# One-core linear attention, mixture of experts and MLP: another opening order, routing sums and one-hots on GpSimd, earlier second gather

## The chip, the cores and the metric

One Trainium2 chip, of which the kernel uses one core. The metric is the device time of one execution in microseconds (us). TensorE (PE) multiplies, VectorE (DVE) and ScalarE (ACT) work on elements and can read the matmul results in PSUM, GpSimd (POOL) works on elements in SBUF and issues the indirect DMAs, SyncE (SP) issues nearly all other DMAs. Each engine takes its instructions in the order in which the program lists them, and a waiting instruction holds back all behind it on that engine or queue.

## The reference

```
proj = x @ w_phi                            # x is q or k; 4 batches, 8 heads, 576 rows, 64 wide
phi(x) = [exp(proj - max|proj|), exp(-(proj - max|proj|))]       # 128 + 128 features
kv = sum_s phi(k)[s] v[s]^T ;  z = sum_s phi(k)[s]
x  = phi(q) @ kv / (phi(q) @ z + 1e-6)      # regrouped to 2304 tokens x 512
noisy  = x @ w_gate + log1p(exp(x @ w_noise)) * noise            # 8 experts
top2   = the two largest of noisy ; weights = softmax over the two
out    = sum over the two experts e of weight * (relu(x @ w1[e]) @ w2[e])   # 512 -> 1024 -> 512
result = max(0.01 h, h) @ w_out,  h = out @ w_in                 # 512 -> 2048 -> 512
```

## The kernel before

**Attention.** It goes by 16 pairs i (a batch b and two of its heads; four pairs are a batch), each over 576 rows as nine tiles in three chunks c. One turn of the main loop (i = 0 to 16) does, in PE's order: `proj` of q (chunk by chunk) and of k for the next pair, as fp16 high and low products into one of three shared PSUM banks (L309, L310, tile `pj`); `kv`, nine tiles per head (L348); transposes of the subtracted q (L334, `tq`); two `fold` products; and the numerators of the pair before (L200, tiles nA, nb). Between them DVE takes the row maximum (L312) and the difference (`shk`, `shq`, L315), ACT the two exponentials `ke` of a k chunk (L327), the copy `kvs` of the finished kv of one head (L356) and the copies `qT`, and DVE divides and forms the gate sums at the pair's end (L410 to L424). The copy `kvs` of head 0 comes once per pair and serves below as the clock of the attention.

**Raw inputs.** q, k and v come as "doubles" of two pairs on SP's queue (`load_double`); the first pair of all comes by itself. Raw q or k of a pair is split into an fp16 high part (`splk`, `splq`: ACT L281, or L294 by thirds) and a low part (POOL L282, or the engine handed in, L295), and then transposed: for most pairs by one DMA on SP's queue (`split_one`, L284, tiles `stkk`, `stkq`), for the first tiles by PE and three ACT copies (`split_pe`, L299, L301).

**Routing.** Per batch a generator `Route` produces the routing in small steps. `tick()` takes the next step of the generator at the head of a list (`flow`); a `yield n` asks for n more ticks before the next step, `PE_NEXT` waits for a place where the routing's own matmuls may stand. The steps are: gate logits and noise scale; the noisy logits `nl` and the top two (`oh`, `ky`, `a`); the ranks of the tokens within their experts (matmuls `pr`, then `re`, `hi`, `lo`); the totals (`pc`, `a_sum`, `bump`, `ebase`); and two tables by one-hot products: for each (tile, choice) pair two one-hots, 128x128 from `lo` (L627) and 128x144 from `hi` (L632), five buffers, then matmuls `pt` (or `o`, L641) that add up which token stands in which slot. Batches 0, 1, 2 are put on the list after turns 4, 8, 12; the last batch is routed during the first steps of the experts. `index_columns` turns table columns into row indices `t_idx`.

**Experts and MLP.** The work is a list of steps s: `mm1` (L963) and `mm2` (L1009), in triples of fp32r high and low products. The first two blocks take the tokens of experts 0 and 1 that are known early. `fetch` gathers 128 rows of x by an indirect DMA on POOL's queue into one of three buffers `xg` (L759); `prep` transposes them (L795) and splits them. The buffers `xg` also hold the hidden values hh and hl of step 0. Weights are split into w0h, w1h (ACT L734) and w0l, w1l (L737: DVE, but the `w1l` of early steps POOL). The order between engines is written out by hand; nothing is scheduled for the author.

Of the kernel before, what the change touches and what calls it, by code (L numbers as in the profile page):

```python
# [26 lines left out]
def attention_moe_mlp_kernel(  # L27
# [259 lines left out]
    def split_pe(nm, i, eng):  # L287
# [14 lines left out]
        stk[nm, i] = x  # L302
# [20 lines left out]
    def k_exp(i, c):  # L323
# [4 lines left out]
        ke[i, c] = e  # L328

# [124 lines left out]
    class Route:  # L454


        def __init__(self, b):
            self.b, self.sb = b, rt_p
            g, odd = divmod(b, 2)
# [56 lines left out]
        def top2(self):  # L516
# [13 lines left out]
            for c in range(2):  # L530
# [5 lines left out]
                nc.vector.tensor_tensor(out=ky, in0=ky,  # L536
# [13 lines left out]
            nc.vector.tensor_tensor(out=a, in0=oh[:, 0], in1=oh[:, 1], op=ALU.add)  # L550
# [3 lines left out]
        def ranks(self):  # L554
# [16 lines left out]
            nc.vector.tensor_tensor(out=oh, in0=oh,  # L571
# [19 lines left out]
        def totals(self):  # L591
# [57 lines left out]
        def weights(self):  # L649
            J, t0 = self.J, self.t0  # L650
            dm = self.small([J], "dm")
            nc.vector.tensor_tensor(out=dm, in0=self.mx[:, 1], in1=self.mx[:, 0],
# [5 lines left out]
            nc.vector.tensor_scalar(out=dm, in0=ex, scalar1=1.0, scalar2=1e-9, op0=ALU.add,  # L658
# [633 lines left out]
```

## Time and profile before

| | us |
|---|---|
| median of 3 runs | 1134.14 (1133.57 to 1135.4) |
| profiled execution | 1134.5 |
| its span in the trace | 1132.7 |
| PE busy in it | 1085.3 (96%) |
| DVE, ACT, POOL busy | 732.6, 542.0, 218.8 |
| mean granted TensorE clock | 0.987 |

The attention ends at about 231 us, the experts and the MLP fill the rest. Times below are microseconds from the start of the span; an instruction's row gives its start and its length, and in brackets how long its engine was idle before it and which instruction ended that.

### The profile page before, as it was taken

Reading aid. Unit: us, or ns where it says so; the run is one execution under the profiler, and the core shown is the slowest. Engines: PE = TensorE matmul, PEld = TensorE weight load, DVE = VectorE, ACT = ScalarE, POOL = GpSimd, SP = SyncE. Lnnn points to the kernel's source line nnn. Section 1 sums busy time; section 2 is a strip of 40 time slices with the busy share of each in tenths; the row PEclk is TensorE's granted clock in tenths of the full one; section 3 lists DMA queues with packets and bytes.
Section 4 is the critical chain, followed back from the end, with each engine's and each line's share of the span. In section 5 each row is a group of like instructions: output and inputs, shape, how many; then the busy total and the mean of one; then the engine's idle time right before and its main releaser. Section 6 shows DMA issues by size and latency. Waiting matters only on the chain. (4 is left out here: it accounts for less than half of the span.)

```text
span 1132.7 us, 18128 instructions
## 1 busy us (share of the span) xinstructions
PE 1085.3 (96%) x6767; PEld 954.9 (84%) x6767; DVE 732.6 (65%) x1558; ACT 542.0 (48%) x1084; POOL 218.8 (19%) x248
## 2 busy tenths in 40 slices
PE   6899899989999999999999999889999999999998
PEld 5899899988888988888888888778888888888886
DVE  4568777779487767676667665576545645645443
ACT  6466455534456444444444454555444444444443
POOL 4121111105434315141413230330000000000000
PEclk9999899989999999999999999899999999999999
DMA  5856462535568636464545462202003003001001
GB/s 136 187 122 152 104 149 43 183 99 176 185 203 253 216 117 206 143 208 147 184 125 200 121 209 76 100 1 94 1 1 112 1 1 110 3 1 32 7 1 37
DMA packets 117001, 125.86 MB, mean 111 GB/s; under 512 B 61040, under 2 KB 87696, under 8 KB 116912
## 3 DMA queue, kind: packets, MB, share of 16 engines
q1 hardware_dynamic: 110320, 104.13, 32.4%
q0 software_dynamic: 6272, 20.03, 5.1%
q8 instruction: 54, 0.88, 0.3%
q10 hardware_dynamic: 320, 0.52, 0.1%
q14 instruction: 35, 0.29, 0.1%
HBM read 96.71 MB, written 19.40 MB: 103 GB/s over the span
## 5 line engine op out<-in xcount | busy, mean ns | idle before, releaser
L963 PE MATMUL m<-xth,w0l 128*128 128x304 f32 (+5 forms) x800 | 268.9, 336 | 3.3 <-issue 3.3
L963 PE MATMUL m<-xth,w0h 128*128 128x304 f32 (+5 forms) x800 | 265.4, 332 | 0.0
L963 PE MATMUL m<-xtl,w0h 128*128 128x304 f32 (+5 forms) x800 | 264.5, 331 | 0.0
L1009 PE MATMUL o<-w1l,hh 128*128 128x512 f32 (+1 forms) x608 | 241.0, 396 | 0.0
L1009 PE MATMUL o<-w1h,hh 128*128 128x512 f32 (+1 forms) x608 | 240.6, 396 | 0.0
L1009 PE MATMUL o<-w1h,hl 128*128 128x512 f32 (+1 forms) x608 | 239.8, 394 | 0.0
L963 PEld LDWEIGHTS m<-xth,w0l 128*128 128x128 f32 x800 | 151.3, 189 | 16.9 <-issue 3.7
L963 PEld LDWEIGHTS m<-xtl,w0h 128*128 128x128 f32 x800 | 151.3, 189 | 13.8
L963 PEld LDWEIGHTS m<-xth,w0h 128*128 128x128 f32 x800 | 151.3, 189 | 10.4
L1009 PEld LDWEIGHTS o<-w1h,hh 128*128 128x128 f32 (+1 forms) x608 | 113.1, 186 | 28.6
L1009 PEld LDWEIGHTS o<-w1h,hl 128*128 128x128 f32 (+1 forms) x608 | 113.1, 186 | 24.3 <-DVE hl L976 0.2
L1009 PEld LDWEIGHTS o<-w1l,hh 128*128 128x128 f32 (+1 forms) x608 | 113.4, 186 | 21.5
L973 DVE SCALAR_TENSOR_TENSOR g<-g 128x512 f32<-128x512 f32 (+1 forms) x80 | 53.4, 668 | 111.7 <-ACT g L972 111.6
L348 PE MATMUL kv<-ke,vs 128*65 128x128 f32 x640 | 121.5, 282 | 0.0
L972 ACT ACTIVATE g<-m 128x512 f32<-128x512 f32 (+1 forms) x80 | 44.4, 555 | 133.1 <-PE m L963 132.8
L734 ACT ACTIVATE w1h<-w2r 128x512 fp32r<-128x512 f32 x88 | 55.4, 630 | 84.0 <-PE o L1009 46.8
L967 DVE SCALAR_TENSOR_TENSOR hl<-m,hh 128x304 fp32r<-128x304 f32 (+4 forms) x128 | 57.9, 471 | 54.4 <-ACT hh L966 53.8
L312 DVE TENSOR_REDUCE m<-pj 128x3 f32<-128x384 f32 x96 | 52.9, 551 | 58.1 <-PE pj L310 57.8
L737 DVE TENSOR_TENSOR w1l<-w2r,w1h 128x512 fp32r<-128x512 f32 x72 | 49.7, 690 | 59.1 <-ACT w1h L734 55.0
L966 ACT ACTIVATE hh<-m 128x304 fp32r<-128x304 f32 (+4 forms) x128 | 50.5, 417 | 72.1 <-PE m L963 70.8
L976 DVE TENSOR_TENSOR hl<-g,hh 128x512 fp32r<-128x512 f32 (+1 forms) x80 | 51.1, 639 | 52.4 <-ACT hh L975 49.8
L975 ACT ACTIVATE hh<-g 128x512 fp32r<-128x512 f32 (+1 forms) x80 | 47.1, 589 | 68.3 <-DVE g L973 68.3
(187 smaller groups left out, 1762.5 us busy)
## 6 DMA issues: line engine op xcount, KB each, us to landing
w1r<-in_moe_w_dram SPq DMA_DIRECT2D x44, 512.0 KB, 4.8
w2r<-in_moe_w_dram SPq DMA_DIRECT2D x44, 512.0 KB, 3.8
y<-y_dram SPq DMA_DIRECT2D x18, 512.0 KB, 6.5
raw<-in_moe_w_in_dram SPq DMA_DIRECT2D x16, 512.0 KB, 4.0
raw<-in_moe_w_out_dram SPq DMA_DIRECT2D x16, 512.0 KB, 4.5
rawk<-in_k_dram SPq DMA_DIRECT2D x16, 256.0 KB, 4.6
vs<-in_v_dram SPq DMA_DIRECT2D x32, 128.0 KB, 3.2
x_dram<-xb SPq DMA_DIRECT2D x4, 1024.0 KB
```

The source lines that it names most:

```text
L312: nc.vector.tensor_reduce(out=m, in_=p, axis=AX, op=ALU.max, apply_absolute_value=True)
L348: nc.tensor.matmul(kvb[:, sg, h], vs[i // 2 % NV][:, i % 2, 5 * h + n], ke[i, t // 3][:, t % 3, sg], start=(n == 0), stop=(n == 4))
L734: nc.scalar.activation(hi, src, ACTF.Copy)
L737: (nc.gpsimd if pool else nc.vector).tensor_tensor(out=lo, in0=src, in1=hi.bitcast(F32), op=ALU.subtract)
L963: nc.tensor.matmul(p, w[:, kk], x[:, kk, c0:c1], start=(kk == 0 and m == 0), stop=(kk == KD - 1 and m == 2))
L966: nc.scalar.activation(hh[:, c0:c1], p, ACTF.Relu)
L967: nc.vector.scalar_tensor_tensor(out=hl[:, c0:c1], in0=p, scalar=0.0, in1=hh[:, c0:c1].bitcast(F32), op0=ALU.max, op1=ALU.subtract)
L972: nc.scalar.activation(g, p, ACTF.Copy)
L973: nc.vector.scalar_tensor_tensor(out=g, in0=g, scalar=0.01, in1=g, op0=ALU.mult, op1=ALU.max)
L975: nc.scalar.activation(hh[:, c0:c1], g, ACTF.Copy)
L976: nc.vector.tensor_tensor(out=hl[:, c0:c1], in0=g, in1=hh[:, c0:c1].bitcast(F32), op=ALU.subtract)
L1009: nc.tensor.matmul(acc[n][0:rows], a[:, c], w, start=(f == 0 and m == 0), stop=(f == nf - 1 and m == 2))
```

## The change

Four things move; the line numbers after the change are a few higher than before.

The opening: `split_pe` becomes a generator that is taken in pieces by `take`. The low part of q of pair 0 goes in front of the first exponentials, the exponentials of the third k chunk of pair 0 go behind the first `kvs` and `qT`, and the low parts of k of pair 1 are POOL's instead of DVE's. The loads of k of pair 1 stay early; the rest of double 1 (raw q, the rest of k, v) now stands in SP's queue behind the DMA transposes of q(1) and k(2). Doubles are loaded one turn-pair later, k is split two pairs ahead instead of three, the noise is loaded in turn 1 instead of 0, and some POOL memsets move into the middle of turn 0.

Routing: two more places that tick (`k_exp`, `kv_evac`) make 23 ticks per turn of 18. For the batches 0 to 2 GpSimd does both one-hots of a pair in one step, and the small sums and products listed in the diff.

Early gathers: the indices of expert 1's early tiles are made after batch 2's routing, and the gather of block 1 reads only the rows of x that batches 0 to 2 write.

```diff
@@ split_pe
+        stk[nm, i] = x
         for w in parts:
             nc.scalar.activation(s[:, w, 0], r[:, w], ACTF.Copy)
             eng.tensor_tensor(out=s[:, w, 1], in0=r[:, w], in1=s[:, w, 0], op=ALU.subtract)
+            yield
         for w in parts:
...
             nc.scalar.activation(x[:, w], p, ACTF.Copy)
-        stk[nm, i] = x
+            yield
@@ k_exp, kv_evac
+        tick()
@@ Route
+            self.eng = nc.gpsimd if b < B - 1 else nc.vector
...
-            nc.vector.tensor_tensor(out=nl, in0=sc, in1=nz[:, t0:t0 + J], op=ALU.mult)
+            self.eng.tensor_tensor(out=nl, in0=sc, in1=nz[:, t0:t0 + J], op=ALU.mult)
             # likewise nl + logits, ky * erev, a, oh * re, hi (two), a_sum +=,
             # max of bump, ebase +=, dm (two), wgt
...
-                nc.vector.tensor_scalar(out=ol, in0=iota[:, 0:128],
+                self.eng.tensor_scalar(out=ol, in0=iota[:, 0:128],
                                         scalar1=self.lo[:, c, j:j + 1], scalar2=None,
                                         op0=ALU.is_equal)
-                yield 0
                 t = self.t0 + j
-                nc.vector.tensor_scalar(out=oi, in0=iota, scalar1=self.hi[:, c, j:j + 1],
+                self.eng.tensor_scalar(out=oi, in0=iota, scalar1=self.hi[:, c, j:j + 1],
                                         scalar2=tokval[:, t, c:c + 1], op0=ALU.is_equal,
                                         op1=ALU.mult)
@@ fetch
-    N_EARLY = tile_of(2, 0)[0] * 128
+    def n_rows(bi):
+        if bi < len(EARLY_TILES):
+            t, p0, n = tile_of(1 + bi, 4)
+            return t * 128 + p0 + n if p0 == 0 else tile_of(2 + bi, 0)[0] * 128
+        return NT
...
-                out=x[0:m], out_offset=None, in_=x_dram[0:N_EARLY] if bi == 0 else x_dram,
+                out=x[0:m], out_offset=None, in_=x_dram[0:n_rows(bi)],
@@ opening
+    load_k(1, 0)
+    load_k(1, 2)
...
-    split_pe("k", 0, nc.vector)
+    k0 = split_pe("k", 0, nc.vector)
+    take(k0, 6)
+    q0 = split_pe("q", 0, nc.gpsimd)
+    take(q0, 3)
     for c in range(2):
         proj("k", 0, c)
-        k_exp(0, c)
-    split_pe("q", 0, nc.gpsimd)
+    k_exp(0, 0)
+    take(q0, 1)
+    k_exp(0, 1)
+    take(q0, 2)
     proj("k", 0, 2)
-    k_exp(0, 2)
     load_gates()
@@ route
-        if b == 1:
-            flow.append([0, index_columns((0, EARLY_TILES[0]))])
+        if b > 0:
+            c = (b - 1) * TPE
+            flow.append([0, index_columns((c, c + EARLY_TILES[b - 1]))])
@@ main loop
             if i == 0:
-                split_pe("k", 1, nc.vector)
-                load_double(1)
+                k_exp(0, 2)
+                k1 = split_pe("k", 1, nc.gpsimd)
+                take(k1, 3)
+                split_one("q", 1)
+                take(k1, 3)
+                load_q(1)
+                split_one("k", 2)
+                load_k(1, 1)
+                for part in range(3):
+                    load_v(1, part)
...
-            split_one("q", 1)
-            split_one("k", 2)
-            load_double(2)
-            load_noise()
-        if i + 3 < NPAIR:
-            split_one("k", i + 3)
+            for n in range(1, NV):
+                make_ones(n, nc.gpsimd)
+            make_pads()
+        if 0 < i < NPAIR - 2:
+            split_one("k", i + 2)
...
-        if i % 2 and (i + 5) // 2 < NPAIR // 2:
-            load_double((i + 5) // 2)
+        if i % 2 and (i + 3) // 2 < NPAIR // 2:
+            load_double((i + 3) // 2)
@@ after the attention
-    flow.append([0, index_columns((TPE, TPE + EARLY_TILES[1]))])
     flow.append([0, iter_fetch(1)])
```

ACT in the opening, before: raw q split (`splq`, three thirds) stands behind four exponentials, all six exponentials of pair 0's k before the first `kvs`, and the splits of q(1), k(2), k(3), q(2) before the second.

```order
L327 ACTIVATE ke<-shk 128x3x128 x4
L294 ACTIVATE splq<-rawq 128x3x64 x3
L301 ACTIVATE stkq<-tr 128x384 x3
L327 ACTIVATE ke<-shk 128x3x128 x2
L356 ACTIVATE kvs<-kv 65x256
L338 ACTIVATE qT_128<-tq 128x3x2x64 x2
L294 ACTIVATE splk<-rawk 128x3x64 x3
L301 ACTIVATE stkk<-tr 128x384 x3
L327 ACTIVATE ke<-shk 128x3x128 x2
L281 ACTIVATE splq<-rawq 128x9x64
L281 ACTIVATE splk<-rawk 128x9x64 x2
L281 ACTIVATE splq<-rawq 128x9x64
```

ACT in the opening, after, from the same place:

```order
L295 ACTIVATE splq<-rawq 128x3x64 x3
L329 ACTIVATE ke<-shk 128x3x128 x2
L303 ACTIVATE stkq<-tr 128x384
L329 ACTIVATE ke<-shk 128x3x128 x2
L303 ACTIVATE stkq<-tr 128x384 x2
L359 ACTIVATE kvs<-kv 65x256
L341 ACTIVATE qT_128<-tq 128x3x2x64 x2
L329 ACTIVATE ke<-shk 128x3x128 x2
L295 ACTIVATE splk<-rawk 128x3x64 x3
L281 ACTIVATE splq<-rawq 128x9x64
L303 ACTIVATE stkk<-tr 128x384 x3
L281 ACTIVATE splk<-rawk 128x9x64
```

The split of q moved ahead of all exponentials, two exponentials moved behind `kvs` and `qT`, and one whole split (q(1)) now stands between the thirds of k(1) and their copies. Behind these rows stand two `ke`, the split of q(2) and the second `kvs`, in both.

SP's queue in the opening, before: all of double 1, the two transposes of q(1) and k(2), then double 2.

```order
L225 DMA rawq<-in_q_dram 128x2x576
L238 DMA rawk<-in_k_dram 128x2x256
L254 DMA vs_123<-in_v_dram 128x4x64 x4
L259 DMA vs_123<-in_v_dram 64x2x64 x2
L284 DMA_TRANSPOSE stkq<-splq 128x9x128
L284 DMA_TRANSPOSE stkk<-splk 128x9x128
L238 DMA rawk<-in_k_dram 128x2x256
L245 DMA rawk<-in_k_dram 64x2x64 x2
```

SP's queue after, from the same place (ahead of it stand the first two loads of k of double 1, in both):

```order
L284 DMA_TRANSPOSE stkq<-splq 128x9x128
L225 DMA rawq<-in_q_dram 128x2x576
L284 DMA_TRANSPOSE stkk<-splk 128x9x128
L238 DMA rawk<-in_k_dram 128x2x256
L254 DMA vs_123<-in_v_dram 128x4x64 x4
L259 DMA vs_123<-in_v_dram 64x2x64 x2
L284 DMA_TRANSPOSE stkq<-splq 128x9x128
L284 DMA_TRANSPOSE stkk<-splk 128x9x128
L284 DMA_TRANSPOSE stkq<-splq 128x9x128
L238 DMA rawk<-in_k_dram 128x2x256
```

The load of the next raw q is now issued after the transpose of q(1), and double 2 (the last row) after three more transposes.

POOL at the end of the attention, before: the gathers of block 0, three `w1l`, then gathers of block 1 among `w1l`.

```order
L759 DMA xg<-x_dram,t_idx 128x512 x2
L737 TENSOR_TENSOR w1l<-w2r,w1h 128x512 x3
L759 DMA xg<-x_dram,t_idx 128x512 x2
L737 TENSOR_TENSOR w1l<-w2r,w1h 128x512
L759 DMA xg<-x_dram,t_idx 128x512
L737 TENSOR_TENSOR w1l<-w2r,w1h 128x512 x4
```

POOL at the same place after, from the last one-hots of batch 2's first table on:

```order
L632 TENSOR_SCALAR hot<-iota,lo 128x128
L636 TENSOR_SCALAR hot<-iota,hi,tokval 128x144
L768 DMA xg<-x_dram,t_idx 128x512 x2
L632 TENSOR_SCALAR hot<-iota,lo 128x128
L636 TENSOR_SCALAR hot<-iota,hi,tokval 128x144
...
L656 TENSOR_TENSOR dm<-mx 128x4
L662 TENSOR_SCALAR dm<-ex 128x4
L667 TENSOR_TENSOR wgt<-ex,wgt 128x4
L768 DMA xg<-x_dram,t_idx 128x512 x3
L741 TENSOR_TENSOR w1l<-w2r,w1h 128x512 x8
```

All three gathers of block 1 moved ahead of the first `w1l`, and the one-hots are new on this engine: 8, 10 and 8 (tile, choice) pairs in the batches 0, 1 and 2, two instructions each. In batch 1 the two low splits of a later pair stand between the two tables; in batch 0 they stand before the first.

## Rows read from the trace of the kernel before

**Rows 1.** The page's busy times: engine, busy us, share, instructions.

```profile
PE 1085.3 (96%) x6767; PEld 954.9 (84%) x6767; DVE 732.6 (65%) x1558; ACT 542.0 (48%) x1084; POOL 218.8 (19%) x248
```

**Rows 2.** Timeline of PE: start, us, instruction, [idle before, what ended it].

```profile
14.05 0.42 PE L348 MATMUL kv<-ke,vs 128*65 128x128 f32 x1
...
22.27 0.42 PE L348 MATMUL kv<-ke,vs 128*65 128x128 f32 x1
...
44.79 0.23 PE L309 MATMUL pj<-wpl,stkq 128*128 128x128 f16 x1 [3.06 <-DVE rd L415]
...
244.32 1.78 PE L641 MATMUL o<-hot 128*128 128x144 f32 x4 [3.48 <-DVE hot L632]
...
261.43 0.44 PE L795 MATMUL t<-ident,xg 128*128 128x128 f32 x2 [1.88 <-DMA xg<-x_dram,t_idx]
```

**Rows 3.** Windows: us, busy (instructions) per engine, granted clock, DMA share, GB/s.

```profile
40.00:50.00 10.00, 6.93 (x60) 6.76 (x58) 6.31 (x20) 3.94 (x9) 1.08 (x2) 0.83 1.00 200
240.00:260.00 20.00, 16.07 (x88) 13.90 (x86) 15.38 (x51) 7.99 (x19) 6.92 (x6) 0.83 0.56 176
```

**Rows 4.** Timeline of ACT: the kvs copies that clock the attention.

```profile
18.23 0.38 ACT L356 ACTIVATE kvs<-kv 65x256 f32<-65x256 f32 x1 [2.45 <-PE kv L348]
...
26.19 0.36 ACT L356 ACTIVATE kvs<-kv 65x256 f32<-65x256 f32 x1
...
51.65 0.38 ACT L356 ACTIVATE kvs<-kv 65x256 f32<-65x256 f32 x1 [4.65 <-PE kv L348]
...
88.98 0.38 ACT L356 ACTIVATE kvs<-kv 65x256 f32<-65x256 f32 x1 [0.87 <-PE kv L348]
...
101.40 0.38 ACT L356 ACTIVATE kvs<-kv 65x256 f32<-65x256 f32 x1 [2.11 <-PE kv L348]
...
147.91 0.38 ACT L356 ACTIVATE kvs<-kv 65x256 f32<-65x256 f32 x1 [0.82 <-PE kv L348]
...
226.90 0.38 ACT L356 ACTIVATE kvs<-kv 65x256 f32<-65x256 f32 x1 [2.10 <-PE kv L348]
```

**Rows 5.** Timeline of ACT in the opening.

```profile
8.48 1.99 ACT L327 ACTIVATE ke<-shk 128x384 f32<-128x384 f32 x4 [1.34 <-DVE shk L315]
10.38 0.85 ACT L294 ACTIVATE splq<-rawq 128x192 f16<-128x192 f32 x3
...
23.05 0.94 ACT L327 ACTIVATE ke<-shk 128x384 f32<-128x384 f32 x2 [1.30 <-DVE shk L315]
...
25.62 0.67 ACT L281 ACTIVATE splq<-rawq 128x576 f16<-128x576 f32 x1
```

**Rows 6.** Timeline of SP's queue.

```profile
40.25 1.50 SPq L284 DMA_TRANSPOSE stkq<-splq  x1
```

**Rows 7.** DMA issues from 0 to 60 us: count, KB each, us to landing.

```profile
rawq<-in_q_dram SPq DMA_DIRECT2D x3, 576.0 KB, 4.6
```

**Rows 8.** Groups of POOL by form: busy us, mean ns of one, idle before.

```profile
L295 POOL TENSOR_TENSOR splq<-rawq,splq 128x192 f16<-128x192 f32 x3 | 1.6, 543 | 7.2 <-DMA vs<-in_v_dram 7.2
L91 POOL IOTA iota<- 128x144 f32 x1 | 0.3, 305 | 0.1
```

**Rows 9.** Timeline of an undisturbed pair (the kvs of 88.98): POOL and PE.

```profile
93.85 1.27 POOL L282 TENSOR_TENSOR splq<-rawq,splq 128x576 f16<-128x576 f32 x1
96.56 0.41 PE L334 MATMUL tq<-ident,shq 128*128 128x128 f32 x2 [0.24 <-DVE mk L540]
```

**Rows 10.** Timelines at the first expert steps: POOL, PE, DVE.

```profile
256.61 0.97 POOL L759 DMA_INDIRECT xg<-x_dram,t_idx  x1 [0.56 <-DVE t_idx L677]
258.87 1.29 POOL L737 TENSOR_TENSOR w1l<-w2r,w1h 128x512 fp32r<-128x512 f32 x1
...
249.83 0.39 PE L1009 MATMUL o<-w1l,hh 128*128 128x512 f32 x1
...
250.52 0.28 PE L963 MATMUL m<-eh,w0l 128*128 128x256 f32 x1
...
251.93 0.57 PE L641 MATMUL o<-hot 128*128 128x144 f32 x4
...
244.29 0.34 DVE L632 TENSOR_SCALAR hot<-iota,hi,tokval 128x144 fp32r<-128x144 f32 x1
```

More of the change, by code (lines that the diff above doesn't have):

```diff
@@ L356, in kv_evac @@
         nc.scalar.activation(kvsb[i][:, h], kvb[:, :, h], ACTF.Copy)
+        tick()
     def fold_mm(i, h):
@@ L521, in top2 @@
             yield 0
-            nc.vector.tensor_tensor(out=nl, in0=sc, in1=nz[:, t0:t0 + J], op=ALU.mult)
+            self.eng.tensor_tensor(out=nl, in0=sc, in1=nz[:, t0:t0 + J], op=ALU.mult)
             yield 0
-            nc.vector.tensor_tensor(out=nl, in0=nl, in1=ln[:, :, 0:E], op=ALU.add)
+            self.eng.tensor_tensor(out=nl, in0=nl, in1=ln[:, :, 0:E], op=ALU.add)
             yield 0
@@ L535, in top2 @@
                 yield 0
-                nc.vector.tensor_tensor(out=ky, in0=ky,
+                self.eng.tensor_tensor(out=ky, in0=ky,
                                         in1=erev.unsqueeze(1).to_broadcast([128, J, E]),
@@ L549, in top2 @@
             a = self.small([J, E], "a", BF16)
-            nc.vector.tensor_tensor(out=a, in0=oh[:, 0], in1=oh[:, 1], op=ALU.add)
+            self.eng.tensor_tensor(out=a, in0=oh[:, 0], in1=oh[:, 1], op=ALU.add)
             self.oh, self.mx, self.a = oh, mx, a
@@ L570, in ranks @@
             yield 0
-            nc.vector.tensor_tensor(out=oh, in0=oh,
+            self.eng.tensor_tensor(out=oh, in0=oh,
                                     in1=re.unsqueeze(1).to_broadcast([128, 2, J, E]),
@@ L579, in ranks @@
             lo = self.small([2, J], "lo")
-            nc.vector.tensor_scalar(out=hi, in0=sl, scalar1=1.0 / 128, scalar2=-63.5 / 128,
+            self.eng.tensor_scalar(out=hi, in0=sl, scalar1=1.0 / 128, scalar2=-63.5 / 128,
                                     op0=ALU.mult, op1=ALU.add)
             yield 0
-            nc.vector.tensor_scalar(out=hi, in0=hi, scalar1=12582912.0, scalar2=-12582912.0,
+            self.eng.tensor_scalar(out=hi, in0=hi, scalar1=12582912.0, scalar2=-12582912.0,
                                     op0=ALU.add, op1=ALU.add)
@@ L600, in totals @@
             else:
-                nc.vector.tensor_tensor(out=a_sum, in0=a_sum, in1=ar, op=ALU.add)
+                self.eng.tensor_tensor(out=a_sum, in0=a_sum, in1=ar, op=ALU.add)
             yield 0
@@ L613, in totals @@
                 yield 0
-                nc.vector.tensor_scalar(out=bump[:, e:e + 1], in0=bump[:, e:e + 1], scalar1=0.0,
+                self.eng.tensor_scalar(out=bump[:, e:e + 1], in0=bump[:, e:e + 1], scalar1=0.0,
                                         scalar2=None, op0=ALU.max)
                 yield 0
-                nc.vector.tensor_tensor(out=ebase[:, e:e + 1], in0=ebase[:, e:e + 1],
+                self.eng.tensor_tensor(out=ebase[:, e:e + 1], in0=ebase[:, e:e + 1],
                                         in1=bump[:, e:e + 1], op=ALU.add)
@@ L651, in weights @@
             dm = self.small([J], "dm")
-            nc.vector.tensor_tensor(out=dm, in0=self.mx[:, 1], in1=self.mx[:, 0],
+            self.eng.tensor_tensor(out=dm, in0=self.mx[:, 1], in1=self.mx[:, 0],
                                     op=ALU.subtract)
@@ L657, in weights @@
             yield 2
-            nc.vector.tensor_scalar(out=dm, in0=ex, scalar1=1.0, scalar2=1e-9, op0=ALU.add,
+            self.eng.tensor_scalar(out=dm, in0=ex, scalar1=1.0, scalar2=1e-9, op0=ALU.add,
                                     op1=ALU.add)
@@ L662, in weights @@
             yield 0
-            nc.vector.tensor_tensor(out=wgt[:, t0:t0 + J, 1], in0=ex, in1=wgt[:, t0:t0 + J, 0],
+            self.eng.tensor_tensor(out=wgt[:, t0:t0 + J, 1], in0=ex, in1=wgt[:, t0:t0 + J, 0],
                                     op=ALU.mult)
@@ L799, in prep, with take @@
         nc.vector.tensor_tensor(out=lo, in0=p, in1=hi.bitcast(F32), op=ALU.subtract)
+    def take(g, n):
+        for _ in range(n):
+            next(g)
     load_k(0, 0)
@@ L809, in attention_moe_mlp_kernel @@
     load_v(0, 1)
+    load_k(1, 0)
+    load_k(1, 2)
     make_split_w_phi()
     make_ones(0, nc.gpsimd)
-    split_pe("k", 0, nc.vector)
+    k0 = split_pe("k", 0, nc.vector)
+    take(k0, 6)
+    q0 = split_pe("q", 0, nc.gpsimd)
+    take(q0, 3)
     for c in range(2):
         proj("k", 0, c)
-        k_exp(0, c)
-    split_pe("q", 0, nc.gpsimd)
+    k_exp(0, 0)
+    take(q0, 1)
+    k_exp(0, 1)
+    take(q0, 2)
     proj("k", 0, 2)
-    k_exp(0, 2)
     load_gates()
-    for i in range(1, NV):
-        make_ones(i, nc.gpsimd)
-    make_pads()
     todo = {}
@@ L1027, in attention_moe_mlp_kernel @@
     pe_ok = False
-    while flow[0][0] != PE_NEXT:
+    while flow and flow[0][0] != PE_NEXT:
         tick()
```

1 line of the change is left out of this document (added).

## The prediction

> **What bounds the kernel now.** I read the page's busy times first: PE is busy for 96% of the span, DVE for 65%, ACT for 48%, POOL for 19% [rows 1]. So the kernel is PE's length, and a change that takes no matmul away can win only PE's idle time and the time in which PE runs at the lower clock. Next I read PE's timeline for the gaps of over 1.5 us; the reader should look at the bracket at a row's end. In the stretch that the change touches stand 3.06 us before 44.79, where PE waits for q's transposed rows, 3.48 before 244.32, where the one-hots of DVE are late, and 1.88 before 261.43, where the first gather of block 1 is late [rows 2]. The windows add what follows the first two: the granted clock is 0.83 over 10 us around the first and over 20 us around the second [rows 3], which at the two levels 1.2 and 2.4 GHz is 3.4 and 6.8 us at the lower one. The same four matmuls take 1.78 us at 244.32 and 0.57 at 251.93 [rows 2, 10]. Behind the gap of 1.88 the clock did not fall: the window that holds it is used up by the 6.8 us. Last I read the copies of kv on ACT as a clock of the attention [rows 4]. From 88.98 to 101.40 a pair takes 12.42 with nothing in its way. From 101.40 to 147.91 three pairs take 46.5 instead of 37.3, an excess of 9.2: batch 0 is routed there. From 147.91 to 226.90 six pairs take 79.0 instead of 74.5, an excess of 4.5.
>
> **The opening.** ACT is idle from 7.14 to 8.48 and then does four exponentials before q's split at 10.38 [rows 5]. After the change the split can start at 7.1, 3.2 sooner; two exponentials (1.0, half of the 1.99) now stand between the copies of q's transposed thirds, so the first kv starts about 2.1 sooner than 14.05 [rows 2], at 11.95, and its copy falls at 16.1 instead of 18.23 [rows 4]. Before the second head's kv, which started at 22.27 [rows 2], ACT now has two exponentials more (0.94) and q(1)'s split (0.67) [rows 5], and POOL makes the low thirds of k(1) at 0.54 each [rows 8], by estimate 0.2 more than DVE: 1.8 in all, so that this kv starts at 21.9, 0.4 sooner. Now the added wait. The split of q(2) on ACT needs the raw q that is loaded behind the DMA transpose of q(1), and that transpose needs POOL's low part of q(1). From 16.1, kvs and qT (1.2), exponentials (0.94), thirds and split (1.5) and POOL's 1.27 [rows 9] put that at 21.0, with handovers at 21.5; the transpose takes 1.5 [rows 6] and the load 4.6 to land [rows 7]: 27.6. Behind the waiting split (0.67) stands the second kvs, which comes at 28.3 instead of 26.19 [rows 4]: 2.1 later; PE waits for it through the fold products. What goes in return is the excess up to kvs of pair 2 at 51.65: from 26.19 that is 25.5 for one and a half pairs, 18.6 undisturbed, so 6.9 too much, the gap of 3.06 and 1.7 lost at the lower clock among it. That gap is due to the queue: the transpose of q(2) stood at 40.25 behind the bulk of double 2 [rows 6], which now comes later. I leave 1.4 of the 6.9 in place: 28.3 + 18.6 + 1.4 = 48.3, a gain of **3.3**. Bounds: 4.7 with nothing left, and a loss of 2.1 if the later wait only moves everything.
>
> **Batch 0's routing.** The small sums leave DVE, and PE's ranks and tables come sooner. Of the excess of 9.2, PE's own work stays: 0.3 for the ranks (estimate) and two table products of 0.57 [rows 10], 1.4 in all. New is a stall. PE's first table product stands between a q projection and the q transposes, 7.6 us after a kvs (96.56 less 88.98 [rows 4, 9]). POOL reaches the one-hots only when its two low splits are done, 95.1 in the undisturbed pair, 6.15 after kvs [rows 9]; two small sums make it 6.7. The first table wants four tile-choice pairs, eight instructions. The trace has no one-hot on POOL. Bounds: at least 0.305, the iota that only writes the same 128x144; at most 0.543, a sum of two inputs over 192 columns [rows 8]. A line through 192 columns (0.543) and 576 columns (1.27 [rows 9]) gives 0.435 at the mean of 128 and 144 columns, and I take it, since it is POOL's own rate. Eight make 3.5, so the table is ready at 10.2 and PE waits 2.6. The excess becomes 4.0, a gain of **5.3** (bounds 4.4 and 6.3 by the two prices).
>
> On DVE the same 128x144 one-hot takes 0.34 [rows 10]. The Trainium skill ("GPSIMD Engine Reference", section 3 "Performance versus the Vector engine") gives GpSimd 1.96 times VectorE's time for an elementwise sum: that would be 0.67 an instruction, and the total below would come out near 1132; its section 4.1 calls operations on one input roughly line rate, by which it would be 0.34 and the total near 1123. No row here shows which holds, and nothing else hangs on this.
>
> **Batches 1 and 2.** Five pairs a table in batch 1: ten one-hots from 6.25 to 10.6, while PE asks at about 7.2, a stall of 3.4. The second table has two splits and ten more one-hots in front, 6.9 by these prices, and half a turn more of time, so I cost it at nothing; the cover is thin. PE's own work is about 2.2: two table products of 0.57, and by estimate as much for ranks and totals. 5.6 against the excess of 4.5 is a loss of **1.1** (bounds: a loss of 2.2 and no loss). Batch 2's tables lie after the last split on POOL, so they should be free.
>
> **The first expert steps.** Batch 2's tables no longer stand between the first steps, so the gap of 3.48 goes, and with it the lower clock: PE worked at it for 5.5 us, from 244.32 until a 512-column product is short again at 249.83 [rows 10], which costs 2.7 at the other level. The gather of block 1 no longer waits for the index of 256.61 [rows 10], so 1.88 goes: 8.1 together. Late next is POOL: its second and third gather of block 1 wait until step 0 gives back their buffers, and the first `w1l` now stands behind both. From 256.61 over two gathers to the end of `w1l` at 260.16 is 3.55 [rows 10]; PE has one first product to do meanwhile, 1.41 (250.52 to 251.93 [rows 10]). That is a new stall of 2.1, a net gain of **6.0** (8.1 if the gathers get away sooner, 4 if the clock falls there).
>
> **The clock at the new gaps.** Gaps of 3.06 and 3.48 were followed by the lower clock, one of 1.88 was not. There are four new ones: about 2 in the opening, 2.6, 3.4 and 2.1. I count two falls of 2.7 each, a loss of **5.4** (bounds 0 and 10.8).
>
> **The sum.** 3.3 + 5.3 - 1.1 + 6.0 - 5.4 = 8.1. The profiled execution took 1134.5 (its span 1132.7 and 1.8 around it), 0.4 over the median: 1126.4 against it, 1126 against the median.
>
> **The rivals.** *GpSimd becomes the bound of the tables (slower).* For: PE's first tables wait for 8 and 10 one-hots in a row, and once the cover is gone for batch 1's second ten, 28 in all. Each 0.1 us more on an instruction then costs 2.8. The gain of 8.1 is eaten at 0.435 + 0.29 = 0.72 an instruction. At 1.0 the sum gives 1142, and at 1.29, which POOL takes for a 128x512 sum with the same fp32r output [rows 10], 1150. Against: POOL's rows follow the size, and 0.72 lies above a sum with two inputs and 192 columns. Chance 0.14.
>
> *Waits change their place only (no change).* Every new gap brings the clock down (10.8 instead of 5.4) and the opening gives nothing (3.3): 1126 + 5.4 + 3.3 = 1135. For: the gap of 3.06 alone cost a fall. Against: three of the four gaps are shorter than those that did it. Chance 0.12.
>
> *Better than forecast.* One-hots at 0.305 (28 x 0.13 = 3.6) and no fall of the clock (5.4): 1117. For: a one-hot has one large input like the iota; the gap of 1.88 cost no clock. Against: the splits before the one-hots stay whatever they cost. Chance 0.20.
>
> **How the numbers follow.** The forecast has 0.54. Faster by over 0.2% (2.3 us, about what a measurement of this kernel can tell) is it and the last rival, 0.74; the same is the second, 0.12; slower the first, 0.14. The range 1115 to 1137 leaves out the far side of the first rival (0.11) and what would come if nearly all gaps closed (0.07).
>
> **What would show it.** In the profile after: the first kvs near 16.1, the second near 28.3, pair 2's near 48.3, and ACT waiting for raw q before q(2)'s split; POOL one-hots between 0.3 and 0.54; PE idle 2.6 and 3.4 before the first tables of batches 0 and 1, and 2.1 at the first `w1l`; no gap before step 0; the lower clock after two of these. Six pairs to the last kvs near 80, the three of batch 0 near 41. One-hots over 0.72, or a second table of batch 1 that waits too, would make the prediction wrong; so would an opening in which later raw loads leave PE idle again at pairs 2 and 3.

## The result, and the profile after

The changed kernel takes 1147.11 us (median of 4 runs, 1142.1 to 1148.03) against 1134.18 before: 1.0104 times as long, 95% interval 1.0073 to 1.0134. The forecast was 1126 with a range of 1115 to 1137, so it was wrong in size and in sign. The profiled execution took 1146.59, its span 1144.4.

The page's busy times of the kernel after, which answer to [rows 1]: TensorE does as many products and is busy for 1087.3 us instead of 1085.3. So of the 11.7 us more of span only 2.0 are busy time, and 9.7 are idle time of TensorE.

```profile
PE 1087.3 (95%) x6767; PEld 954.0 (83%) x6767; DVE 712.2 (62%) x1464; ACT 541.4 (47%) x1084; POOL 265.5 (23%) x342
```

The clock of the kvs copies, to be held against [rows 4] (timeline of ACT after; the first two rows are pair 0's heads, then head 0 of pairs 2, 6, 9, 12 and 15):

```profile
13.74 0.38 ACT L359 ACTIVATE kvs<-kv 65x256 f32<-65x256 f32 x1 [2.39 <-PE kv L351]
...
26.41 0.36 ACT L359 ACTIVATE kvs<-kv 65x256 f32<-65x256 f32 x1
...
49.35 0.38 ACT L359 ACTIVATE kvs<-kv 65x256 f32<-65x256 f32 x1 [2.20 <-PE kv L351]
...
100.02 0.38 ACT L359 ACTIVATE kvs<-kv 65x256 f32<-65x256 f32 x1 [1.79 <-PE kv L351]
...
147.21 0.38 ACT L359 ACTIVATE kvs<-kv 65x256 f32<-65x256 f32 x1
...
196.42 0.38 ACT L359 ACTIVATE kvs<-kv 65x256 f32<-65x256 f32 x1 [4.62 <-PE kv L351]
...
240.22 0.38 ACT L359 ACTIVATE kvs<-kv 65x256 f32<-65x256 f32 x1 [2.31 <-PE kv L351]
```

Pair 2 comes 2.3 sooner than the 51.65 of before. Of that, 0.9 are lost up to pair 6 and 0.7 more up to pair 9 (147.21 against 147.91, with 0.7 left). From there to pair 15 it takes 93.0 instead of 79.0: 14.0 lost in the six pairs in which batches 1 and 2 are routed. The rest to the end takes 904.2 instead of 905.8. So 2.3 - 0.9 - 0.7 - 14.0 + 1.6 makes the loss of 11.7.

Windows over these pairs (us, busy of PE, PEld, DVE, ACT, POOL, granted clock, DMA share, GB/s) show what they consist of: first pairs 6 to 9 and 9 to 15 before, then the same two after.

```profile
101.40:147.91 46.51, 41.52 (x414) 40.02 (x413) 36.21 (x104) 23.07 (x54) 7.56 (x6) 0.93 0.53 126
147.91:226.90 78.99, 75.45 (x817) 73.69 (x816) 61.57 (x218) 44.47 (x105) 13.40 (x11) 1.00 0.47 120
```

```profile
100.02:147.21 47.19, 41.67 (x414) 40.01 (x413) 28.22 (x80) 22.88 (x53) 19.68 (x25) 0.93 0.47 111
147.21:240.22 93.01, 80.83 (x823) 78.14 (x822) 56.35 (x184) 45.11 (x107) 37.42 (x62) 0.94 0.50 122
```

In pairs 9 to 15 TensorE is idle for 12.2 us instead of 3.5 and busy for 5.4 longer, and the granted clock falls from 1.00 to 0.94. In pairs 6 to 9 neither its idle time (5.0 and 5.5) nor its clock (0.93) got better, though VectorE has 8.0 us less to do.

What TensorE waits for in that part, and which products it stands at. First two lines from the list of its waits from 95 to 245 us (what waits, for what: us in total, times, longest), then its timeline:

```profile
PE pt L645 <- POOL hot L636: 7.1, 8, 1.1
PE pr L563 <- POOL a L555: 2.7, 1, 2.7
```

```profile
109.00 0.30 PE L645 MATMUL pt<-hot 128*128 128x144 f32 x1 [0.78 <-DVE shq L317]
110.24 0.33 PE L645 MATMUL pt<-hot 128*128 128x144 f32 x1 [0.93 <-POOL hot L636]
111.66 0.49 PE L645 MATMUL pt<-hot 128*128 128x144 f32 x1 [1.08 <-POOL hot L636]
113.07 0.49 PE L645 MATMUL pt<-hot 128*128 128x144 f32 x1 [0.93 <-POOL hot L636]
...
177.17 0.64 PE L645 MATMUL pt<-hot 128*128 128x144 f32 x4 [0.34 <-POOL hot L636]
178.53 0.34 PE L645 MATMUL pt<-hot 128*128 128x144 f32 x1 [0.71 <-POOL hot L636]
...
186.21 0.36 PE L645 MATMUL pt<-hot 128*128 128x144 f32 x1 [1.08 <-POOL hot L636]
187.62 0.49 PE L645 MATMUL pt<-hot 128*128 128x144 f32 x1 [1.06 <-POOL hot L636]
189.04 0.49 PE L645 MATMUL pt<-hot 128*128 128x144 f32 x1 [0.93 <-POOL hot L636]
...
219.30 0.18 PE L563 MATMUL pr<-a,upper 128*128 128x32 bf16 x1 [2.69 <-POOL a L555]
```

TensorE takes one product, waits about 1 us for the next one-hot, takes the next. Windows around these pauses show the lower clock that comes with them: 0.83 over 20 us twice and 0.89 over 15 us, which is 6.8, 6.8 and 3.3 us at 1.2 GHz.

```profile
100.00:120.00 20.00, 15.92 (x139) 14.96 (x139) 9.32 (x29) 7.66 (x17) 14.63 (x21) 0.83 0.36 75
180.00:200.00 20.00, 16.93 (x154) 16.33 (x153) 8.32 (x30) 7.11 (x17) 8.98 (x12) 0.83 0.59 120
215.00:230.00 15.00, 11.43 (x108) 11.06 (x107) 9.01 (x33) 5.45 (x13) 1.87 (x8) 0.89 0.84 250
```

The first of the three is not new. The kernel before has as long a stretch in these pairs (0.93 over 46.51 us is 6.5 at 1.2 GHz), in which its first table of batch 0 stands (timeline of PE before):

```profile
123.16 0.83 PE L641 MATMUL pt<-hot 128*128 128x144 f32 x4 [1.32 <-DVE shk L315]
```

So the other two, 10.1 us at 1.2 GHz, are what the change added in pairs 9 to 15; half of that is lost.

The one-hots on GpSimd, groups by form (busy us, mean ns of one, idle before), where the prediction took 435 ns for either:

```profile
L636 POOL TENSOR_SCALAR hot<-iota,hi,tokval 128x144 fp32r<-128x144 f32 x26 | 22.2, 854 | 0.0
L632 POOL TENSOR_SCALAR hot<-iota,lo 128x128 fp32r<-128x128 f32 x26 | 15.8, 606 | 0.3 <-DVE lo L591 0.3
```

It looked like the first rival. The first experiments took that apart.

### The profile page after: what moved, and what is told of

Read it like the earlier page. It is cut to its first block, busy times and chain, and to the rows that moved or that the text cites. A ratio compares the mean times of both kernels' runs of the same rounds, so it can differ in the third digit from the quotient of the medians.

```text
span 1144.4 us, 18138 instructions
## 1 busy us (share of the span) xinstructions
PE 1087.3 (95%) x6767; PEld 954.0 (83%) x6767; DVE 712.2 (62%) x1464; ACT 541.4 (47%) x1084; POOL 265.5 (23%) x342
## 5 line engine op out<-in xcount | busy, mean ns | idle before, releaser
L988 PEld LDWEIGHTS m<-xth,w0h 128*128 128x128 f32 x800 | 150.6, 188 | 10.5
L738 ACT ACTIVATE w1h<-w2r 128x512 fp32r<-128x512 f32 x88 | 55.4, 630 | 88.3 <-PE o L1034 49.2
L741 DVE TENSOR_TENSOR w1l<-w2r,w1h 128x512 fp32r<-128x512 f32 x72 | 49.7, 690 | 59.6 <-ACT w1h L738 53.1
L1108 POOL TENSOR_TENSOR cm<-ce,cm 128x512 f32<-128x512 f32 x32 | 41.6, 1300 | 178.6 <-ACT cm L1107 178.5
L991 ACT ACTIVATE hh<-m 128x304 fp32r<-128x304 f32 (+4 forms) x128 | 50.6, 418 | 65.3 <-PE m L988 61.4
```

The source lines that it names most:

```text
L738: nc.scalar.activation(hi, src, ACTF.Copy)
L741: (nc.gpsimd if pool else nc.vector).tensor_tensor(out=lo, in0=src, in1=hi.bitcast(F32), op=ALU.subtract)
L988: nc.tensor.matmul(p, w[:, kk], x[:, kk, c0:c1], start=(kk == 0 and m == 0), stop=(kk == KD - 1 and m == 2))
L991: nc.scalar.activation(hh[:, c0:c1], p, ACTF.Relu)
L1108: nc.gpsimd.tensor_tensor(out=m, in0=e.bitcast(F32), in1=m, op=ALU.mult)
```

## The experiments

All times are medians; the ratio is to the kernel before on the same chip, with its 95% interval. It is worked out over all runs of both and is not the quotient of the two medians. Stages below are differences of kvs starts, us of span in the one profiled execution of each kernel; those of e6 and e14 took 4.2 and 2.7 us more than the median of their kernels, that of e8 2.6 less.

| kernel | to pair 2 | 2-6 | 6-9 | 9-12 | 12-15 | 15 to end | ratio |
|---|---|---|---|---|---|---|---|
| before | 51.7 | 49.7 | 46.5 | 39.1 | 39.8 | 905.8 | 1 |
| after | 49.3 | 50.7 | 47.2 | 49.2 | 43.8 | 904.2 | 1.0104 (1.0073 to 1.0134) |
| e1 one-hots on DVE | 50.2 | 50.7 | 51.0 | 47.7 | 44.8 | 905.6 | 1.0159 (1.0129 to 1.0188) |
| e2 small steps on DVE | 49.4 | 50.7 | 47.0 | 49.1 | 44.7 | 903.9 | 1.0133 (1.0106 to 1.0160) |
| e3 all on DVE | 50.1 | 50.7 | 47.9 | 47.5 | 45.0 | 904.5 | 1.0125 (1.0099 to 1.0150) |
| e4 opening only | 50.1 | 49.7 | 46.7 | 39.1 | 39.9 | 906.2 | 1.0006 (0.9991 to 1.0021) |
| e5 no added ticks | 49.8 | 49.8 | 42.6 | 47.0 | 40.4 | 905.3 | 1.0026 (1.0011 to 1.0041) |
| e6 ticks only | 51.0 | 50.7 | 45.1 | 43.3 | 44.2 | 905.3 | 1.0031 (1.0016 to 1.0047) |
| e7 as e5, all on DVE | 49.0 | 49.7 | 44.5 | 44.3 | 44.1 | 904.9 | 1.0036 (1.0010 to 1.0063) |
| e8 one tick place | 47.7 | 50.1 | 44.6 | 41.3 | 40.9 | 908.1 | 1.0036 (1.0023 to 1.0048) |
| e9 more cover | 48.2 | 50.7 | 40.7 | 42.1 | 46.4 | 907.0 | 1.0056 (1.0037 to 1.0074) |
| e10 before, ticks and one step | 51.6 | 50.7 | 50.6 | 45.9 | 43.0 | 904.8 | 1.0128 (1.0091 to 1.0165) |
| e11 two steps | 51.0 | 50.7 | 41.6 | 43.7 | 45.0 | 901.3 | 1.0022 (1.0008 to 1.0035) |
| e12 e5 and cover | 50.6 | 49.8 | 42.6 | 39.0 | 40.0 | 910.0 | 1.0005 (0.9993 to 1.0018) |
| e13 e12, batch 2 on DVE | 50.4 | 49.8 | 41.1 | 39.0 | 40.0 | 907.9 | 0.9967 (0.9953 to 0.9982) |
| e14 e12, all on DVE | 50.8 | 49.7 | 44.8 | 39.9 | 40.3 | 907.2 | 0.9989 (0.9972 to 1.0006) |

In pairs 2 to 6 every row with 23 ticks a turn has 50.7, e8 with 20 has 50.1, and every row with 18 has 49.7 or 49.8: the 0.9 lost there comes with the ticks.

**Whose price is it? (e1 to e4)**

e1, only the one-hots back on VectorE:

```diff
-                self.eng.tensor_scalar(out=ol, in0=iota[:, 0:128],
+                nc.vector.tensor_scalar(out=ol, in0=iota[:, 0:128],
...
-                self.eng.tensor_scalar(out=oi, in0=iota, scalar1=self.hi[:, c, j:j + 1],
+                nc.vector.tensor_scalar(out=oi, in0=iota, scalar1=self.hi[:, c, j:j + 1],
```

> The changed kernel with only the one-hots of batches 0 to 2 back on VectorE; GpSimd keeps the small sums and products. Theory G (one-hots on GpSimd are dear: 0.61 and 0.86 us in the trace after, 1.46 a pair, and TensorE waits for them): TensorE's waits for one-hots (3.7 us at 108 to 113, 4.1 at 177 to 189) go, and with them the two stretches of 6.8 us at the lower clock behind them (3.4 each): 14.6 less than 1146.6, so 1132 (1129 to 1136). Theory W (the loss comes from the small steps that hop between VectorE and GpSimd and queue behind the splits): the hops stay, at most the 7.8 us of waits go and new ones come with VectorE's load: 1140 or more.

Measured 1151.37: theory G falls, and W is not shown by it.

e2, the reverse: every `self.eng.` but those two becomes `nc.vector.`.

> The changed kernel with the small sums and products back on VectorE and only the one-hots on GpSimd. Theory G: little is won, the wait for a (2.7) and a_sum (0.6) and the lower clock behind them (1.7) at most: 1141 to 1147. Theory W: the loss against the kernel before goes, 1134 or less.

Measured 1147.36: W falls too.

e3, all routing on VectorE:

```diff
-            self.eng = nc.gpsimd if b < B - 1 else nc.vector
+            self.eng = nc.vector
```

> The changed kernel with all routing steps back on VectorE, but with the new opening, 23 ticks a turn and the early gathers. If G and W together are the whole loss, the terms that the prediction got right are left: opening 2.4, first expert steps some 2 to 6, and part of the 5.3 of batch 0's routing: 1124 to 1130. Rival (VectorE becomes the bound when the same work comes in fewer turns: it is busy 27 us of 40 in undisturbed pairs): 1134 or more, with waits of TensorE for VectorE in turns 5 to 7 and 9 to 12.

Measured 1147.29, as with GpSimd. That is the rival's time, but TensorE waits at the same places as with GpSimd, now for VectorE (waits of TensorE from 95 to 245 us in e3):

```profile
PE pt L645 <- DVE hot L636: 3.6, 6, 1.0
PE pr L563 <- DVE a L555: 2.9, 1, 2.9
```

The wait for `a` is 2.9 with no GpSimd in it and 2.7 with GpSimd. So moving the work to the other engine does not take the loss away. That VectorE is now the bound, as the rival says, e3 by itself does not refute; e9 to e11 below leave the engines as they are and move the order.

e4, the opening alone: the opening and load order of the kernel after, with the routing, ticks and gathers of the kernel before.

> The kernel before with the new opening and load order alone: routing, ticks and gathers as before. The clock of kvs copies in the trace after stands 2.4 us earlier at pair 2: theory that this gain is kept gives 1131.8 (1130 to 1133). Rival (the later loads and splits delay GpSimd or the transposes in later pairs, which took 50.7 instead of 49.8 from pair 2 to pair 6): 1133 to 1136.

Measured 1133.34 against 1131.44, a ratio of 1.0006 with 1 inside its interval: no difference shown. The trace has pair 2 1.6 sooner and the span 0.9 shorter than the trace before. A gain of 2.4 would be a ratio of 0.998, which lies outside the interval; nor does the opening hurt later pairs. One execution says little here: in the thirteen rows with this opening pair 2 comes between 47.7 and 51.0.

**Pace (e5 to e8)**

e5, without the two added tick places; e7 is the same with e3's edit:

```diff
@@ k_exp, kv_evac
-        tick()
```

> The changed kernel without the two added tick places (18 ticks a turn as before; GpSimd, one step per one-hot pair, opening and gathers stay). After the first four runs theories G and W stand badly: with all routing on VectorE the time is 1147 as well. New theory P (pace): with 23 ticks the routing's matmuls stand a half to a whole turn earlier in TensorE's order, before their inputs can be ready, whichever engine makes them, and TensorE waits in order; then this run falls from 1147 to 1134 or less (12 less at the least). Rival X (the one step per pair, the early index and gather, or the order of GpSimd): 1143 or more.

Measured 1136.73 against 1133.58: between the two forecasts, nearer to that of theory P. Ten of the thirteen us are gone, so the added ticks are part of the cause. By stages pairs 9 to 12 still lose 7.9, and 5.7 are won up to pair 9.

e6, the kernel before with the two `tick()` added:

> The kernel before with the two added tick places and nothing else. Theory P: at least two thirds of the loss, 1140 or more against about 1132 of the kernel before, with a TensorE wait before the ranks of batch 2 in turn 14 (2.7 to 2.9 in the traces so far) and waits for one-hots in turn 7. Rival X: 1134 or less.

Measured 1137.3 against 1133.58: slower by 3.7, under a third of the loss where theory P asked for two thirds, and more than rival X allowed. So neither P nor X holds as it stood.

> The changed kernel without the two added tick places and with all routing steps on VectorE. TensorE's order is that of the run without ticks, so the difference between the two is GpSimd's alone. Theory P: 1134 or less, as the run without ticks. If GpSimd's price of 1.46 us a one-hot pair matters at this pace (theory G, what is left of it), this one is 4 or more faster than that run.

Measured 1138.58, its ratio within the interval of e5: again the engine decides nothing that shows in the sum.

e8, only the tick behind `kvs`:

> The changed kernel with one of the two added tick places (behind kvs: 20 ticks a turn). Theory P says the loss comes with the distance in TensorE's order: between the run without ticks and 1147, about 1137 to 1142. If the place of the tick decides and not the pace (the three ticks behind the exponentials), as fast as the run without ticks.

Measured 1137.44, not told apart from e5, so it does not decide between the two readings.

What e5 and e6 have in common with the kernel after can be counted in TensorE's order, where a turn has 89 matmuls besides the routing's own (a product of `kv`, `fold` or the numerators counts once; the trace has two records of each). Counted is how many stand between the total `pc` of batch 1 and its first table, and between the first and the second.

| | pc to first table | first to second |
|---|---|---|
| before | 89 | 89 |
| after, e3, e10 | 46 | 43 |
| e5, e7 | 49 | 83 |
| e6, e11 | 79 | 56 |
| e8 | 83 | 46 |
| e9 | 89 | 79 |
| e12, e13, e14 | 89 | 83 |

Both edits shorten it: more ticks a turn, and one step instead of two a one-hot pair. In between, the one-hots have to be made. The loss does not follow from one count alone: e8, with 46 before the second table, loses 2.2 in pairs 9 to 12, and e5, with 49 before the first, 7.9.

**Cover (e9 to e12)**

e10, the kernel before with both edits, the opening, VectorE and gathers as before:

```diff
@@ k_exp, kv_evac
+        tick()
@@ table
                                         op0=ALU.is_equal)
-                yield 0
                 t = self.t0 + j
```

> The kernel before with the two tick places and one step per one-hot pair, nothing else: opening, VectorE for all routing and the gathers of before. Its routing matmuls stand in TensorE's order where the changed kernel has them. Theory C: the whole loss, 1143 to 1149, though each of the two edits alone cost 3 to 5. Rival (the loss needs GpSimd or the new opening): 1140 or less, the sum of the two.

Measured 1148.7 against 1132.7. That is the whole loss, without GpSimd, opening or early gathers. It is spread otherwise: pairs 6 to 9, 9 to 12 and 12 to 15 lose 4.1, 6.8 and 3.2 here, and 0.7, 10.1 and 4.0 in the kernel after. Waits of TensorE from 95 to 245 us in e10:

```profile
PE pt L642 <- DVE hot L633: 3.6, 6, 1.0
PE pj L309 <- DVE shk L315: 2.4, 3, 1.5
PE pr L560 <- DVE a L552: 2.3, 1, 2.3
```

e11, the reverse in the kernel after: the `yield 0` between the two one-hots of a pair put back.

> The changed kernel with two steps per one-hot pair as before, still on GpSimd and with 23 ticks. TensorE's order of the routing becomes that of the kernel before with ticks only (1137). Theory C: 1135 to 1140. Rival G (1.46 us a pair on GpSimd is the price wherever it stands): 1144 or more.

Measured 1135.08 against 1132.7, with every one-hot still on GpSimd and 23 ticks: 1.0022 instead of 1.0104. The one-hots have left the head of the list of TensorE's waits (95 to 245 us in e11); `a`, whose place did not move, is still there:

```profile
PE pr L563 <- POOL a L555: 2.7, 1, 2.7
PE pj L311 <- ACT qT L341: 1.6, 2, 1.0
PE tq L337 <- DVE mx L536: 1.5, 2, 0.8
```

e9, more ticks of cover in the kernel after:

```diff
-            yield 4
+            yield 4 if self.b > 1 else 12
             yield PE_NEXT
...
             elif not ps_m:
-                yield 2
+                yield 8
```

> The changed kernel (23 ticks, GpSimd, opening and gathers as changed) with more cover: 12 ticks instead of 4 between a table's last one-hot and its matmuls for the batches 0 and 1, and 8 instead of 2 before the ranks of batch 2; nothing else moves. Theory C (what costs is the distance in TensorE's order between a routing step and the matmul that needs it): the waits for one-hots of batches 0 and 1 (3.7 and 4.1 in the trace after), most of the wait for a (2.7) and the lower clock behind them go: 1133 to 1138. Rival L (the load of GpSimd or the earlier place of the ranks as such): 1143 or more.

Measured 1138.83, just above the range of theory C and below its rival's. Pairs 6 to 9 take 40.7 and 9 to 12 42.1, but pairs 12 to 15 take 46.4: there the total `pc` now waits longest. The ranks of batch 2 were moved back and `pc` was not moved as far, so that 43 matmuls stand between them instead of 64 (TensorE's waits from 95 to 245 us in e9):

```profile
PE pc L613 <- POOL a_sum L606: 2.4, 2, 1.8
```

This fits theory C if cover has to stand before each product that moves; no run gave `pc` its cover back.

e12, e5 with cover for the one table that still lacked it:

```diff
-            yield 4
+            yield 11 if self.b == 1 and keys[0][1] == 0 else 4
             yield PE_NEXT
```

> The changed kernel without the two tick places and with 7 ticks more before the first table of batch 1, the one place where the run without ticks still lost (47.0 us for pairs 9 to 12 against 39.1 before, while pairs 6 to 9 took 42.6 against 46.5). Theory C by stages of the traces: 49.8 + 49.8 + 42.6 + 39.1 + 40.4 + 905.3 = 1127 of span, so 1129 (1126 to 1132) against about 1133 before. If the cover isn't what that place lacks: 1135 or more.

Pairs 9 to 12 fall from 47.0 to 39.0, as theory C says, but the time is 1133.52 against 1132.7: 910.0 from pair 15 on instead of the 905.3 of the sum. There batch 2's first table lies among the first expert steps, 28 matmuls behind its total `pc` where e5 has 47, and TensorE waits for its one-hots (timeline of PE in e12):

```profile
239.77 0.49 PE L643 MATMUL o<-hot 128*128 128x144 f32 x1 [1.08 <-POOL hot L634]
241.18 0.49 PE L643 MATMUL o<-hot 128*128 128x144 f32 x1 [0.93 <-POOL hot L634]
242.60 0.49 PE L643 MATMUL o<-hot 128*128 128x144 f32 x1 [0.93 <-POOL hot L634]
```

**GpSimd's part (e13, e14)**

e13, e12 with `nc.gpsimd if b < B - 2`, so that batch 2 is VectorE's; e14, e12 with e3's edit.

> The run without ticks and with 7 ticks of cover, but with batch 2's routing on VectorE (its tables lie between the first expert steps, where the trace of that run shows waits for one-hots of GpSimd of 2.5, 1.1, 0.9, 0.9, 0.9 and 1.1). Theory: GpSimd's price of 1.46 a pair counts exactly where no cover stands, so that stage falls back to its length before, 905.8 from the last pair on instead of 910.0, with pairs 2 to 15 as in that run: span 1128, time 1129 to 1131, faster than both kernels (about 3 under before). Rival: VectorE's load delays the same tables as much: 1133 as that run.

Measured 1129.82 (12 runs) against 1132.88: 0.9967 times, faster than both kernels, with a span of 1128.1. The stage after pair 15 is 907.9, 2.1 less than in e12, half of the 4.2 expected. Pairs 6 to 9, which the edit leaves as they were, took 41.1 instead of 42.6, so of the stages of one execution 1.5 is scatter (TensorE is idle for 2.75 us there in both, but the granted clock was 1.00 in e13 and 0.96 in e12); the ratio over all runs is what stands, and its interval lies clear of e12's.

> The same order with all routing on VectorE. If GpSimd helps where the cover is there (pairs 6 to 9 took 42.6 with it and 44.5 without, in the two runs without ticks), this one is 2 to 3 slower than the run before it, about 1132 to 1134; if the engine doesn't matter at all, the same.

Measured 1132.06 against 1132.88. Its ratio lies 0.0022 above e13's, and the intervals just overlap; seven of its twelve runs took longer than the longest of e13's twelve. By stages it loses 3.7 in pairs 6 to 9 (44.8 against 41.1), where batch 0's one-hots have cover and GpSimd takes them off VectorE. But only 0.6 of the 3.7 are idle time of TensorE; the rest goes with the lower clock (windows over these pairs in e13, then in e14):

```profile
100.20:141.28 41.08, 38.33 (x414) 37.26 (x413) 28.36 (x81) 22.97 (x54) 20.09 (x27) 1.00 0.57 138
```

```profile
100.54:145.32 44.78, 41.43 (x414) 40.04 (x413) 35.00 (x104) 22.84 (x53) 7.54 (x6) 0.92 0.52 125
```

That GpSimd helps there is likely; how much of it is the engine and how much the clock of one execution is not shown.

## Why the prediction was wrong

**The step that failed is batches 1 and 2**, forecast as a loss of 1.1 and measured as 14.0. It had TensorE ask at 7.2 us after a kvs and stall for 3.4 before the first table of batch 1. TensorE asked at 176.83, GpSimd had begun the one-hots at 171.34, and the stall was only 1.05 (0.34 and 0.71). The second table, for which it saw "half a turn more of time" and so put the wait "at nothing", shows 3.07 (1.08, 1.06, 0.93). The half turn was there (43 of 89 matmuls), but TensorE was through it in 5.7 us, from 178.87 to 184.58. The prediction had put 6.9 of GpSimd's work against half a turn, which is 6.2 in an undisturbed pair, and still took the wait as nothing. GpSimd took 10.5 from the end of the first table's one-hots, 178.48 to 188.98 (timeline of POOL after):

```profile
171.34 0.62 POOL L632 TENSOR_SCALAR hot<-iota,lo 128x128 fp32r<-128x128 f32 x1
...
177.61 0.87 POOL L636 TENSOR_SCALAR hot<-iota,hi,tokval 128x144 fp32r<-128x144 f32 x1
179.38 1.28 POOL L282 TENSOR_TENSOR splk<-rawk,splk 128x576 f16<-128x576 f32 x1 [0.91 <-ACT splk L281]
...
188.13 0.85 POOL L636 TENSOR_SCALAR hot<-iota,hi,tokval 128x144 fp32r<-128x144 f32 x1
```

And batch 2, which "should be free" because its tables lie behind the last split, waits 2.7 for `a` before its ranks, an instruction that the prediction never placed. What it didn't weigh for either batch is how few matmuls the new order leaves between a routing step and the product that needs it; e10 and e11 show that this order carries the loss. Of the 14.0, 8.6 are idle time, and most of the other 5.4 are the 10.1 us at 1.2 GHz. A second table of batch 1 that waits was among the signs that the prediction had named as making it wrong.

**Batch 0's routing**, forecast as a gain of 5.3, lost 0.7. The stall was 3.7 (0.78, 0.93, 1.08, 0.93) for 2.6. The deeper fault is in both terms: the excess of 9.2 in pairs 6 to 9 was read as work that goes with VectorE's load. The trace before has 5.0 us of idle TensorE in it and 3.3 lost at the lower clock, and after the change both are as large, with 8.0 us less on VectorE. With the order nearer to that of before and GpSimd at work (e5) the stage falls by 3.9, and by 2.0 with the same order on VectorE (e7). So at most 1.9 are GpSimd's, little more than the scatter of one execution. The change also brings the products nearer to their inputs, and I read the earlier place of a matmul as a gain.

**The price of a one-hot** was 0.73 on the mean instead of 0.435, beyond the upper bound of 0.543 and just above the 0.72 from which the first rival decides and which was another of the named signs. It lengthens the stalls where GpSimd makes the one-hots: the second table's ten took 7.1 and not 4.35. That rival still does not explain the loss: it gives 1135 at this price, and e3 and e10 reach 1147 and 1149 without GpSimd. Where no cover stands the price does count (e12 to e13).

**Rightly forecast** were the shape of the opening and that TensorE stalls at `w1l`. The first kvs came at 13.74 (forecast 16.1), the second at 26.41 (28.3), pair 2 at 49.35 (48.3), and ACT waits for raw q as the added wait says. Of the gain of 3.3 the trace shows 2.3 at pair 2, and e4 shows none in the time. Timelines of ACT, PE and POOL after:

```profile
25.82 0.68 ACT L281 ACTIVATE splq<-rawq 128x576 f16<-128x576 f32 x1 [5.20 <-DMA rawq<-in_q_dram]
```

```profile
262.61 0.51 PE L1034 MATMUL o<-w1l,hh 128*128 128x512 f32 x1 [2.08 <-POOL w1l L741]
```

```profile
257.71 1.03 POOL L768 DMA_INDIRECT xg<-x_dram,t_idx  x1 [0.69 <-DVE u L690]
```

The stall of 2.1 was measured as 2.08, but that the size fits is partly luck. The prediction had the first gather of block 1 early and two late ones in front of the `w1l`. The trace has all three late, the first at 257.71 behind a wait for VectorE, where before it stood at 256.61. And of the 6.0 that the first expert steps should win only 1.6 came: the gaps of 3.48 and 1.88 are gone, and smaller ones for the last batch's routing came in return:

```profile
258.83 0.39 PE L988 MATMUL m<-eh,w0l 128*128 128x256 f32 x1 [0.72 <-DVE w0l L741]
...
267.38 0.18 PE L563 MATMUL o<-a,upper 128*128 128x40 bf16 x1 [1.28 <-DVE a L555]
```

Which of them takes how much of the 4.4 that are missing was not tried, and no run has the early gathers alone. The 0.9 lost in pairs 2 to 6 was not forecast at all.

**The clock**, two falls forecast for four new gaps, fell three times in the routing (6.8, 6.8 and 3.3 us at 1.2 GHz, half of which is lost), one of them as before the change. In pairs 6 to 9 the gaps before the fall were of about 1 us each, in a row: single length, as I had argued it, is not what the rows go by. The trace before could have told: the prediction went by the falls behind 3.06 and 3.48 and left out the one in pairs 6 to 9, with no gap over 1.32 in its timeline between 101 and 148 us.

## What to carry to other kernels

Where a schedule is written by counting steps, a faster pace doesn't only bring work forward, it also takes away the instructions that stand between a producer and its matmul; count these on the engine that goes in order, before and after, for every product that moves, and read the producer's whole chain against them. Test the engine and the order apart: here three runs that only changed the engine all kept the loss, and one run that only changed the order had all of it. An engine with a dear instruction costs time where there is no cover (e12 against e13); that it wins time where there is cover is likely here, but not shown. And split a stage's excess into idle time, time at the lower clock and work before calling any of it a gain to come.

## What the runs showed of the hardware

A `tensor_scalar` with its scalars from SBUF is dear on GpSimd: 606 ns for 128 columns with one operation and 854 for 144 with two, where a sum of two inputs over 192 columns takes 543 [rows 8] and VectorE's one-hot 0.34 [rows 10]. The Trainium skill ("GPSIMD Engine Reference", section 4.1 "Engine selection") calls operations with one input roughly line rate there. The rows do not bear that out for this instruction: the 854 are 2.5 times VectorE's 0.34 for the same 128x144.

The same instruction on VectorE is held up while GpSimd runs a split. In e3 it takes 1.21 and 1.33 in place of 0.27 and 0.34 (timeline of DVE, then of POOL):

```profile
122.53 1.21 DVE L632 TENSOR_SCALAR hot<-iota,lo 128x128 fp32r<-128x128 f32 x1
123.67 1.33 DVE L636 TENSOR_SCALAR hot<-iota,hi,tokval 128x144 fp32r<-128x144 f32 x1
124.91 0.27 DVE L632 TENSOR_SCALAR hot<-iota,lo 128x128 fp32r<-128x128 f32 x1
```

```profile
122.38 1.27 POOL L282 TENSOR_TENSOR splk<-rawk,splk 128x576 f16<-128x576 f32 x1 [15.43 <-ACT splk L281]
123.62 1.27 POOL L282 TENSOR_TENSOR splq<-rawq,splq 128x576 f16<-128x576 f32 x1
```

GpSimd's end at 123.65 and 124.89, VectorE's right behind them at 123.74 and 125.00. The Trainium skill ("SBUF — State Buffer", section "SBUF: two separate sides") describes an exclusive lock on a port pair that the two engines share, held for a whole instruction. These rows agree with it. It concerns two of the 52 one-hot instructions that VectorE takes over in e3, some 1.9 us in all, so it does not explain why moving the one-hots between the two engines changed so little.
